# One core of Trainium2: the first ten tiles' work of an attention, MoE and gated-product chain issued in another order

## The chip, the cores and the metric

The kernel runs on one core of one Trainium2 chip. The metric is the device time of one execution in microseconds (us); a smaller one is better. The engines are PE (matrix products and transposes; PEld is its weight load), DVE (the vector engine), ACT (the scalar engine), POOL (GpSimd) and SP, which issues most of the transfers. Each of them takes its instructions strictly in the order in which they were handed to it; semaphores tie the engines to each other.

## The reference, cut to what matters

```
kv  = einsum('bhsd,bhse->bhde', k, v)            # 4 batches, 8 heads, 576 rows, head 64
out = einsum('bhsd,bhde->bhse', q, kv)
x   = out / sqrt(mean(out*out) + 1e-6) * g_norm  # per row and head; x is then 2304 x 512
h   = x @ w_in                                   # 512 -> 1024
e   = exp(h - max(h)); solu = h * e / (sum(e) + 1e-9)
y   = layer_norm(solu) * g_ln @ w_out            # 1024 -> 512
return (y @ w_a * (y @ w_b)) @ w_out2            # 512 -> 1536 -> 512
```

## The kernel before, in words

The 2304 rows are 18 tiles of 128. A first stage makes y of all tiles, two more stages (lines 733 and 905) make the gated product and the output by seven products for eight block products. Products run in a format that keeps fewer bits than float32, so each operand is kept as a high part (a cast on ACT) and a low part (the difference, on DVE or POOL), and each product is three matmuls: high by high, high by low, low by high.

The first stage handles tile i in steps, each a short function that issues instructions to one or two engines:

- `kv_product` (token kp, lines 358 and 363) multiplies k and v of a pair of heads on PE; `kv_keep` copies the result out of PSUM, on DVE (kk) or ACT (ka). There are 16 pairs, 4 for each batch; b0.2 means pair 2 of batch 0.
- `q_turn`, `q_keep` (qt, qk, lines 382, 387) transpose q on PE and copy it out on ACT; `o_product` (op, line 396) is q by kv. `o_square` (ACT, line 407), `o_rms` (line 413 on DVE, then ten small instructions on POOL) and `o_scale` (DVE, line 423) make x.
- `x_turn` (PE, line 433), `x_hi` (ACT, line 438) and `x_lo` (DVE, line 443) give x transposed in its two parts.
- `h_product` (hp, lines 462 to 464): 24 matmuls for h, into the one PSUM buffer `ph`. For tile 0 it is cut into eight pieces h0 to h7, one for each block of w_in, h0 to h3 for the first 512 columns and h4 to h7 for the others. `h_max` (DVE, line 469), `h_exp` (ACT, line 475) and `h_solu` (DVE, lines 480 to 484) read `ph`, and only when `h_solu` is done may the next tile's product write it. `h_square` (ACT), `h_norm` (DVE, then POOL) finish the norm.
- `l_turn`, `l_hi`, `l_lo` (PE, ACT, DVE; lines 518, 528, 531) transpose that result, and `y_product` (yp, lines 548 to 550) is w_out by it for two tiles together.

Beside them the weights are narrowed from a 64-bit format. A block rN of 128 x 512 comes by DMA (`fetch`) into one of five places of `ring`; `begin` (token B, or BP where the clamp goes to POOL) reads it on ACT (line 77); `mid` (M for one block, MM for two) runs the clamp and three more DVE instructions for each (lines 82, 97, 103, 108) and then fetches a further block; `end` makes high part and low part, the low one on POOL (token E) or DVE (EV), line 65. Blocks r1 to r8 are w_in, r9 to r16 w_out (tiles `woh`, `wol`), the rest goes to DRAM for the later stages.

What sets the order of all this is a list of tokens. `PROLOGUE` holds the tokens of tiles 0 to 4 and the front of the following ones, interleaved by hand; `+2` means the tile two later. From tile START on, a fixed list `SLOT` (from tile 10 on `LATER`) is run once for each tile.

```python
    run(PROLOGUE)
    for i in range(START, NTILE - 2):
        run(SLOT if i < 10 else LATER, i)
```

Of the kernel before, what the change touches and what calls it, by code (L numbers as in the profile page):

```python
# [21 lines left out]

START = 5
PROLOGUE = """
LK LW B LW M LQ BP LK LK kp B MM EV LW qt kp LN qk LQ kp LW ka EV ka LQ EV B kk M LQ kp ka BP op LK
os B om qt+1 M E B MM E qk+1 op+1 E os+1 ox qt+2 LQ qt+3 xt qk+2 LK xh E op+2 xl B om+1 M qk+3 os+2
EV om+2 ox+1 LK h0 h1 LQ h2 h3 h4 h6 h5 h7 xt+1 BP xh+1 qt+4 kp hm kp xl+1 op+3 he os+3 B ox+2 hs hq
LQ xt+2 LQ B LK LG xh+2 om+3 hn LK MM xl+2 ka hp+1 hm+1 B kp kp ox+3 ka qk+4 he+1 kk ka op+4 qt+5  # L30
hs+1 lt0 xt+3 os+4 qk+5 lh0 om+4 hp+2 E hq+1 E MM ll0 qt+7 lt1 ox+4 hn+1 hm+2 xh+3 LW BP LK lh1 qt+6
he+2 kp xl+3 op+5 hs+2 B kp os+5 hq+2 om+5 hp+3 qk+6 MM hn+2 LK B LQ xt+4 E ka qk+7 kp ka lt0+1 E
lt1+1 xh+4 hm+3 xl+4 he+3 op+6 lh1+1 ox+5 ll1 lh0+1 B hs+3 ll0+1 lt1+2 ka MM os+6 ll1+1 E EV lh1+2
lt0+2 hp+4 BP xt+5 om+6 B EV EV hq+3 lh0+2 hm+4 he+4 ox+6 hn+3 xh+5 yp yp yp xl+5 hs+4 yp ll1+2
ll0+2 hq+4 lt0+3 hn+4 LK B yk lt1+3 lh0+3 yk M yk M ll0+3 lh1+3 ll1+3 BP E yk
"""
SLOT = """
hp hm lt0-1 lt1-1 lh0-1 lh1-1 ll0-1 ll1-1 xt+1 xh+1 xl+1 op+2 he os+2 yp yk hs hq om+2 kp kk qt+3
# [77 lines left out]
def tile_attention_moe(ctx, tc, q, k, v, g_norm, w_in, w_out, g_ln, w_a, w_b, w_out2, out):  # L116
    nc = tc.nc
    B, H, S, D = q.shape
# [4 lines left out]
    NK = DM // P  # L123
# [36 lines left out]
    left, top, right, late, psum = (ExitStack() for _ in range(5))  # L160
# [121 lines left out]
    def fetch():  # L282
        if fetches:
            src = fetches.pop(0)
            n = len(raws_at) % 5
            raws_at.append(n)
            r = ring[n // 3][:, n % 3 * DM:(n % 3 + 1) * DM]
            nc.sync.dma_start(out=r.rearrange("p (k f) -> p k f", k=NK) if len(src.shape) == 3 else r, in_=src)
            raws.append(r)
# [4 lines left out]
    def begin(on_pool=False):  # L294
        if jobs and raws:
            _, put, args = jobs.pop(0)
            n = Narrow(nc, raws.pop(0), cv.tile([P, DM], U32, tag="u", name="nu"))
            if on_pool:
                n.clamp(nc.gpsimd)
            begun.append((n, put, args))  # L300

    def mid(count=1):
        now = [begun.pop(0) for _ in range(min(count, len(begun)))]
        Narrow.finish([n for n, _, _ in now])
        for n, put, args in now:
# [61 lines left out]
    def kv_keep(copy=nc.vector.tensor_copy):  # L367
        if kvps:
            b, hp, pk = kvps.pop(0)
            for n in range(2):  # L370
                ns = slice(n * D, (n + 1) * D)
                copy(kvb[b % 3][ns, hp, ns], pk[ns])
            ready.add((b, hp))
# [37 lines left out]
    def o_rms(i, eng=nc.gpsimd):  # L411
        ss = sm.tile([P, H], F32, name="ss")
        nc.vector.tensor_reduce(out=ss, in_=sqs.pop(i), op=ALU.add, axis=AX.X)
        ms = sm.tile([P, H], F32, name="ms")
        nc.vector.tensor_scalar(out=ms, in0=ss, scalar1=1.0 / D, scalar2=1e-6, op0=ALU.mult, op1=ALU.add)
        rms[i] = rsqrt(ms, H, "a", eng)

    xt = {}
# [31 lines left out]
    hs_ = {}  # L450

    def h_product(i, part=slice(None)):
        if i not in hs_:
            hs_[i] = dict(ps=ps_h.tile([P, 2, HALF], F32, tag="h", name="ph"))
            hs_[i]["ph"] = hs_[i]["ps"].rearrange("p a b -> p (a b)")
        ph = hs_[i]["ps"]
        xh, xl = xT[i]
        order = [(n, c) for n in range(2) for c in range(NK)]
        order = order if i == 0 else sorted(order, key=lambda nc_: nc_[1])
        for n, c in order[part]:  # L460
            wh, wl = wi[n, c]
            nc.tensor.matmul(ph[:, n, :], xh[:, c, :], wh, start=(c == 0), stop=False)  # L462
            nc.tensor.matmul(ph[:, n, :], xh[:, c, :], wl, start=False, stop=False)  # L463
            nc.tensor.matmul(ph[:, n, :], xl[:, c, :], wh, start=False, stop=(c == NK - 1))  # L464

    def h_max(i):
        d = hs_[i]
# [46 lines left out]
    def l_turn(i, n):  # L514
        pt = ps_t.tile([P, 4, P], F32, tag="t", name="ltp")
        for m in range(4):
            f = 4 * n + m
            nc.tensor.transpose(pt[:, m, :], hs_[i]["so"][:, f * P:(f + 1) * P], ident)  # L518
        psum_of["l", i, n] = pt
# [7 lines left out]
    def l_hi(i, n):  # L527
        nc.scalar.copy(l_part(i, n, 0), psum_of["l", i, n])

    def l_lo(i, n):  # L530
        nc.vector.tensor_tensor(
            out=l_part(i, n, 1), in0=psum_of.pop(("l", i, n)), in1=l_part(i, n, 0).bitcast(F32), op=ALU.subtract
        )
        if (i, n) == ((i // G1 + 1) * G1 - 1, 1):
            pend.extend((i // G1, c) for c in range(NK))
# [476 lines left out]
    def load_gl(_):  # L1012
# [57 lines left out]
    i = NTILE - 2  # L1070
# [8 lines left out]
    i = NTILE - 1  # L1079
# [38 lines left out]
    for n, (count, which) in enumerate(((1, now), (6, later), (5, now), (2, later))):  # L1118
# [3 lines left out]
        for _ in range(count):  # L1122
            part, n = which.pop(0)
# [18 lines left out]
    for j in range(1, NJ - 1):  # L1142
        n = 2 * j + 2
# [181 lines left out]
```

## Time and profile before

| what | value |
|---|---|
| time, median of 3 runs | 688.7 us (688.04 to 689.72) |
| span of the profiled execution, first to last instruction | 686.5 us |
| PE busy in it | 660.6 us, 96% |
| DVE, ACT, POOL busy | 519.4, 283.5, 274.6 us |
| granted PE clock, mean | 0.995 of full |
| chain that ended last, share of PE | 87% |

The page shows one execution, whose time outside the profiler isn't listed apart; its span is 2.2 us under the median of the runs. Of the span cut into 40 equal slices, PE is busy in tenths `3789999999999999999999999999999999999998`: the idle time lies at the front. A wait is put down to the instruction that ended it.

### The profile page before, as it was taken

How to read it: one execution, taken by the hardware profiler on the slowest of the kernel's cores; microseconds unless marked ns; L12 is line 12 of the kernel's file. 1: busy time of each engine (PE TensorE's matmuls, PEld its weight loads, DVE VectorE, ACT ScalarE, POOL GpSimd, SP SyncE). 2: the span in 40 equal slices, each digit the busy share in tenths (PEclk: the TensorE clock that was granted, in tenths of full speed). 3: DMA queues.
4: the chain of work that ended last, by engine and by line, in shares of the span. 5: the costliest groups of instructions: out<-in, count | busy, mean ns of one | idle time of the engine just before them, and what ended most of it. 6: DMA issues, size and time to landing. Idle time of an engine off the chain costs nothing.

```text
span 686.5 us, 12566 instructions
## 1 busy us (share of the span) xinstructions
PE 660.6 (96%) x4710; PEld 634.1 (92%) x4710; DVE 519.4 (76%) x930; ACT 283.5 (41%) x493; POOL 274.6 (40%) x444
## 2 busy tenths in 40 slices
PE   3789999999999999999999999999999999999998
PEld 2668798999999999999999999999999999999997
DVE  4889977675688877879666777686767989978882
ACT  3558854444455346543321122221222545433531
POOL 2667554555534411314564466554672230000000
PEclk9899999999999999999999999999999999999999
DMA  9994745445542412342434346545344784644521
GB/s 304 320 298 137 212 126 182 135 134 161 162 135 70 147 47 70 108 139 89 145 113 150 108 120 199 161 139 150 108 129 135 268 273 141 187 124 139 150 74 62
DMA packets 111100, 103.84 MB, mean 151 GB/s; under 512 B 29248, under 2 KB 98368, under 8 KB 111040
## 3 DMA queue, kind: packets, MB, share of 16 engines
q1 hardware_dynamic: 104992, 94.40, 45.5%
q10 hardware_dynamic: 6048, 8.65, 3.8%
q8 instruction: 37, 0.61, 0.4%
q14 instruction: 23, 0.19, 0.1%
HBM read 71.05 MB, written 31.98 MB: 150 GB/s over the span
## 4 chain that ended last, share of the span: by engine, by line
PE 87%; DVE 5%; DMA 3%; issue 1%; ACT 1%; POOL 1%; SPq 1%; DVEq 0%; ACTq 0%; POOLq 0%
PE pw L733 37%; PE pq L905 19%; PE x2p L550 5%; PE x2p L548 5%; PE x2p L549 5%; PE ph L462 4%; PE ph L463 4%; PE ph L464 4%; DMA ring<-in_moe_w_in_dram 2%; PE ltp L518 2%; PE po L396 2%; PE qtp L382 1%; DMA qs<-in_q_dram 1%; PE xtp L433 1%; DVE nu L103 1%
## 5 line engine op out<-in xcount | busy, mean ns | idle before, releaser
L733 PE MATMUL pw<-xh,wh 128*128 128x384 f32 x336 | 112.9, 336 | 0.8 <-DVE b L785 0.5
L733 PE MATMUL pw<-xh,wl 128*128 128x384 f32 x336 | 112.7, 335 | 0.0
L733 PE MATMUL pw<-xl,wh 128*128 128x384 f32 x336 | 112.6, 335 | 0.0
L775 POOL TENSOR_TENSOR a<-b,a 128x384 f32<-128x384 f32 x53 | 64.4, 1229 | 120.3 <-DVE b L764 120.3
L733 PE MATMUL pw<-x,wh 128*128 128x384 f32 x336 | 85.5, 335 | 0.0
L548 PE MATMUL x2p<-lh,woh 128*128 128x256 f32 x288 | 82.4, 286 | 0.0
L550 PE MATMUL x2p<-lh,wol 128*128 128x256 f32 x288 | 80.4, 279 | 0.8 <-DVE wol L65 0.8
L549 PE MATMUL x2p<-ll,woh 128*128 128x256 f32 x288 | 80.3, 279 | 0.0
L733 PEld LDWEIGHTS pw<-xh,wh 128*128 128x128 f32 x336 | 63.1, 188 | 1.5 <-DVE b L785 0.8
L733 PEld LDWEIGHTS pw<-xl,wh 128*128 128x128 f32 x336 | 63.1, 188 | 0.0
L733 PEld LDWEIGHTS pw<-xh,wl 128*128 128x128 f32 x336 | 63.1, 188 | 0.0
L733 PEld LDWEIGHTS pw<-x,wh 128*128 128x128 f32 x336 | 60.6, 188 | 0.0
L462 PE MATMUL ph<-wih,xh 128*128 128x512 f32 x144 | 56.8, 395 | 2.0 <-DVE so L484 1.8
L905 PE MATMUL pq<-wo,gh 128*128 128x256 f32 x336 | 57.7, 276 | 0.0
L463 PE MATMUL ph<-wil,xh 128*128 128x512 f32 x144 | 56.3, 391 | 0.2 <-DVE wil L65 0.2
L464 PE MATMUL ph<-wih,xl 128*128 128x512 f32 x144 | 56.2, 391 | 0.1
L733 PE MATMUL pw<-x,wl 128*128 128x384 f32 x168 | 56.2, 335 | 0.0
L550 PEld LDWEIGHTS x2p<-lh,wol 128*128 128x128 f32 x288 | 54.5, 189 | 1.2 <-DVE wol L65 1.2
L548 PEld LDWEIGHTS x2p<-lh,woh 128*128 128x128 f32 x288 | 54.2, 188 | 0.3 <-ACT xh L438 0.2
L549 PEld LDWEIGHTS x2p<-ll,woh 128*128 128x128 f32 x288 | 54.2, 188 | 0.0
L905 PE MATMUL pq<-wo,gw 128*128 128x256 f32 x450 | 53.1, 276 | 0.0
L905 PEld LDWEIGHTS pq<-wo,gw 128*128 128x128 f32 x450 | 52.0, 188 | 0.0
(160 smaller groups left out, 1504.0 us busy)
## 6 DMA issues: line engine op xcount, KB each, us to landing
gd<-a SPq DMA_DIRECT2D x72, 192.0 KB, 2.0
ring<-in_moe_w_out_dram SPq DMA_DIRECT2D x20, 512.0 KB, 5.1
gl<-gd SPq DMA_DIRECT2D x14, 384.0 KB, 3.3
gw<-gd SPq DMA_DIRECT2D x12, 384.0 KB, 3.2
ks<-in_k_dram SPq DMA_DIRECT2D x8, 512.0 KB, 5.8
vs<-in_v_dram SPq DMA_DIRECT2D x8, 512.0 KB, 6.3
ring<-in_moe_w_in_dram SPq DMA_DIRECT2D x8, 512.0 KB, 7.4
qs<-in_q_dram SPq DMA_DIRECT2D x16, 256.0 KB, 6.3
```

What stands on the lines that cost most here:

```text
L103: self.nc.vector.scalar_tensor_tensor(out=self.u, in0=self.high, scalar=0xC0000000, in1=self.u, op0=ALU.bitwise_and, op1=ALU.bitwise_or)
L396: nc.tensor.matmul(po[a:a + n, 2 * hp:2 * hp + 2, :], qT[i][:, hp, a:a + n], kvb[b % 3][:, hp, :], start=True, stop=True,)
L462: nc.tensor.matmul(ph[:, n, :], xh[:, c, :], wh, start=(c == 0), stop=False)
L463: nc.tensor.matmul(ph[:, n, :], xh[:, c, :], wl, start=False, stop=False)
L464: nc.tensor.matmul(ph[:, n, :], xl[:, c, :], wh, start=False, stop=(c == NK - 1))
L518: nc.tensor.transpose(pt[:, m, :], hs_[i]["so"][:, f * P:(f + 1) * P], ident)
L548: nc.tensor.matmul(pa, wh[:, cs], lh[:, f, :], start=(f == 0), stop=False)
L549: nc.tensor.matmul(pa, wh[:, cs], ll[:, f, :], start=False, stop=False)
L550: nc.tensor.matmul(pa, wl[:, cs], lh[:, f, :], start=False, stop=(f == NF1 - 1))
L733: nc.tensor.matmul(out, wt_[:, wn, c], xt_[xn][:, c], start=first and c == n == 0, stop=c == 1 and n == 2, skip_group_check=not first,)
L775: eng.tensor_tensor(out=a[n], in0=by, in1=a[n], op=ALU.mult)
L905: nc.tensor.matmul(ps, xt_[:, c], wt_[:, c], start=first and c == n == 0, stop=c == NJ - 1 and n == 2, skip_group_check=not first,)
```

## The change

The token list `PROLOGUE` is a new one that runs up to tile 9 (START is 10), so that `SLOT` is no longer used; the steps themselves are the same and each runs as often as before. The list can't be read for what it moves, so a line of it stands for all. In `h_product` the first matmul on each half of `ph` clears it and the last one closes it, whichever blocks these are, because the new list takes tile 0's pieces as h0 h3 h1 h6 h2 h4 h5 h7.

```diff
-START = 5
+START = 10
 PROLOGUE = """
-LK LW B LW M LQ BP LK LK kp B MM EV LW qt kp LN qk LQ kp LW ka EV ka LQ EV B kk M LQ kp ka BP op LK
+LK LW B LW BP M LK LQ kp LK EV B LW LN qt qk kp MM LQ LW ka EV kp ka EV kk kp B M LQ LQ ka BP op os
...
+        left_ = hs_[i].setdefault("left", [NK, NK])
         for n, c in order[part]:
             wh, wl = wi[n, c]
-            nc.tensor.matmul(ph[:, n, :], xh[:, c, :], wh, start=(c == 0), stop=False)
+            nc.tensor.matmul(ph[:, n, :], xh[:, c, :], wh, start=(left_[n] == NK), stop=False)
             nc.tensor.matmul(ph[:, n, :], xh[:, c, :], wl, start=False, stop=False)
-            nc.tensor.matmul(ph[:, n, :], xl[:, c, :], wh, start=False, stop=(c == NK - 1))
+            left_[n] -= 1
+            nc.tensor.matmul(ph[:, n, :], xl[:, c, :], wh, start=False, stop=(left_[n] == 0))
```

The line numbers of the changed kernel are 8 higher up to `h_product` and 10 higher behind it.

First place, ACT, from tile 0's square (`sq`) on. Block r6 is `nu_290` before and `nu_313` after, r7 `nu_323` and `nu_321`, r8 `nu_388` and `nu_378`; the first `qT` is tile 1's, `xh` is tile 0's. Before:

```order
L407 ACTIVATE sq_288<-po_279 128x512
L77 ACTIVATE nu_290<-ring_114 128x512
L64 CAST wih0_3_319<-nu_252 128x512
L77 ACTIVATE nu_323<-ring_114 128x512
L64 CAST wih1_0_335<-nu_276 128x512
L387 COPY qT_339<-qtp_310 128x512
L64 CAST wih1_1_346<-nu_290 128x512
L407 ACTIVATE sq_350<-po_341 128x512
L387 COPY qT_371<-qtp_354 128x512
L438 ACTIVATE xh_375<-xtp_366,gn_136 128x512
L64 CAST wih1_2_377<-nu_323 128x512
L77 ACTIVATE nu_388<-ring_114 128x512
```

And of the change:

```order
L415 ACTIVATE sq_284<-po_279 128x512
L72 CAST wih0_3_309<-nu_263 128x512
L85 ACTIVATE nu_313<-ring_114 128x512
L395 COPY qT_315<-qtp_286 128x512
L85 ACTIVATE nu_321<-ring_114 128x512
L72 CAST wih1_0_323<-nu_276 128x512
L415 ACTIVATE sq_349<-po_337 128x512
L395 COPY qT_356<-qtp_342 128x512
L72 CAST wih1_1_358<-nu_313 128x512
L85 ACTIVATE nu_378<-ring_114 128x512
L446 ACTIVATE xh_382<-xtp_362,gn_136 128x512
L72 CAST wih1_2_384<-nu_321 128x512
```

Tile 1's `qT` went ahead of the read of r7, and the read of r8 ahead of tile 0's `xh`; r7's high part stays behind `xh`.

Second place, DVE, behind the narrowing of r6 and r7, around the first tile's `x` and `xl`. Before:

```order
L108 SCALAR_TENSOR_TENSOR nu_323<-ring_114,nu_323 128x512
L423 TENSOR_TENSOR x_352<-po_279,y_a_296 128x512
L443 SCALAR_TENSOR_TENSOR xl_386<-xtp_366,gn_136,xh_375 128x512
L413 TENSOR_REDUCE ss_390<-sq_350 128x8
L415 TENSOR_SCALAR ms_392<-ss_390 128x8
L210 TENSOR_SCALAR y_a_394<-ms_392 128x8
L82 TENSOR_SCALAR nu_388<-nu_388 128x512
```

And of the change:

```order
L116 SCALAR_TENSOR_TENSOR nu_321<-ring_114,nu_321 128x512
L431 TENSOR_TENSOR x_347<-po_279,y_a_295 128x512
L73 TENSOR_TENSOR wil1_2_385<-nu_321,wih1_2_384 128x512
L451 SCALAR_TENSOR_TENSOR xl_390<-xtp_362,gn_136,xh_382 128x512
L421 TENSOR_REDUCE ss_408<-sq_349 128x8
L423 TENSOR_SCALAR ms_410<-ss_408 128x8
L218 TENSOR_SCALAR y_a_412<-ms_410 128x8
L90 TENSOR_SCALAR nu_378<-nu_378 128x512
```

The low part of r7 came from POOL, and stands on DVE between `x` and `xl`.

Third place, DVE, from the last narrowing instruction ahead of tile 3's `h_max` (`nm`) to tile 3's `h_solu` (`so`). Before:

```order
L108 SCALAR_TENSOR_TENSOR nu_836<-ring_115,nu_836 128x512
L501 TENSOR_SCALAR va_909<-vs_851 128x1
L210 TENSOR_SCALAR y_l_911<-va_909 128x1
L469 TENSOR_REDUCE nm_975<-ph_871 128x1
L443 SCALAR_TENSOR_TENSOR xl_977<-xtp_931,gn_136,xh_973 128x512
L423 TENSOR_TENSOR x_988<-po_825,y_a_857 128x512
L531 TENSOR_TENSOR ll_696<-ltp_769,lh_695 128x4x128
L480 TENSOR_SCALAR rs_994<-se_980 128x1
L481 RECIPROCAL rs_994<-rs_994 128x1
L484 SCALAR_TENSOR_TENSOR so_997,su_998<-ph_871,rs_994,e_979 128x1024
```

And of the change:

```order
L116 SCALAR_TENSOR_TENSOR nu_867<-ring_115,nu_867 128x512
L73 TENSOR_TENSOR wol2_942<-nu_533,woh2_941 128x512
L479 TENSOR_REDUCE nm_946<-ph_869 128x1
L73 TENSOR_TENSOR wol3_951<-nu_578,woh3_950 128x512
L431 TENSOR_TENSOR x_966<-po_818,y_a_842 128x512
L541 TENSOR_TENSOR ll_697<-ltp_782,lh_696 128x4x128
L451 SCALAR_TENSOR_TENSOR xl_989<-xtp_935,gn_136,xh_978 128x512
L490 TENSOR_SCALAR rs_991<-se_986 128x1
L491 RECIPROCAL rs_991<-rs_991 128x1
L494 SCALAR_TENSOR_TENSOR so_994,su_995<-ph_869,rs_991,e_985 128x1024
```

Two low parts of w_out (r11 and r12) came from POOL; ahead of this piece a kv copy-out and one more clamp came to DVE too, and the small `va` and `y_l` moved further ahead.

## Rows read from the trace of the kernel before

**Rows 1.** Busy time by stretch: us, then PE, PEld, DVE, ACT, POOL, granted clock, DMA

```profile
core 0: us, PE busy (x) PEld busy (x) DVE busy (x) ACT busy (x) POOL busy (x), PEclk, DMA share, GB/s
0.00:37.00 37.00, 19.90 (x148) 16.48 (x148) 23.93 (x45) 17.05 (x32) 18.65 (x38) 0.91 0.97 307
37.00:90.00 53.00, 48.57 (x402) 41.52 (x402) 48.30 (x100) 38.91 (x75) 34.82 (x92) 1.00 0.67 198
90.00:540.00 450.00, 449.72 (x2953) 434.50 (x2953) 329.70 (x627) 166.97 (x298) 210.80 (x310) 1.00 0.44 133
```

**Rows 2.** Waits of PE from 37 to 90 us: engine, line, waited for, us, times, longest

```profile
PE ph L462 <- DVE so L484: 1.8, 3, 0.9
PE xtp L433 <- DVE x L423: 0.9, 1, 0.9
PE x2p L550 <- DVE wol L65: 0.8, 1, 0.8
```

**Rows 3.** Timeline of PE to 37 us: start, us, instruction, idle before and what ended it

```profile
22.19 1.09 PE L382 MATMUL qtp<-ident,qs 128*128 128x128 f32 x4 [2.89 <-DMA qs<-in_q_dram]
...
30.91 0.50 PE L464 MATMUL ph<-wih,xl 128*128 128x512 f32 x1
...
34.88 0.39 PE L463 MATMUL ph<-wil,xh 128*128 128x512 f32 x1
...
36.46 0.50 PE L463 MATMUL ph<-wil,xh 128*128 128x512 f32 x1 [0.23 <-DVE wil L65]
```

**Rows 4.** Timeline of ACT, 23 to 31 us

```profile
23.42 0.68 ACT L77 ACTIVATE nu<-ring 128x512 f32<-128x512 f32 x1 [1.72 <-DMA ring<-in_moe_w_in_dram]
...
24.50 0.59 ACT L387 COPY qT<-qtp 128x512 f32<-128x512 f32 x1
...
29.97 0.61 ACT L64 CAST wih<-nu 128x512 fp32r<-128x512 f32 x1
```

**Rows 5.** Timeline of DVE, 27 to 39 us

```profile
27.68 0.69 DVE L423 TENSOR_TENSOR x<-po,y_a 128x512 f32<-128x512 f32 x1
30.11 0.75 DVE L443 SCALAR_TENSOR_TENSOR xl<-xtp,gn,xh 128x512 fp32r<-128x512 f32 x1 [1.73 <-ACT xh L438]
...
31.48 1.10 DVE L415 TENSOR_SCALAR ms<-ss 128x8 f32<-128x8 f32 x1
32.62 0.17 DVE L210 TENSOR_SCALAR y_a<-ms 128x8 int32<-128x8 int32 x1
...
35.72 0.69 DVE L65 TENSOR_TENSOR wil<-nu,wih 128x512 fp32r<-128x512 f32 x1 [0.69 <-ACT wih L64]
...
37.95 1.22 DVE L469 TENSOR_REDUCE nm<-ph 128x1 f32<-128x1024 f32 x1
```

**Rows 6.** Timeline of DVE, 50 to 60 us

```profile
50.19 0.45 DVE L372 COPY kvb<-kvp 64x64 f32<-64x64 f32 x2
...
53.61 0.76 DVE L82 TENSOR_SCALAR nu<-nu 128x512 f32<-128x512 f32 x2
...
58.99 1.21 DVE L469 TENSOR_REDUCE nm<-ph 128x1 f32<-128x1024 f32 x1
```

**Rows 7.** Timeline of PE, 63 to 84 us

```profile
63.37 0.47 PE L462 MATMUL ph<-wih,xh 128*128 128x512 f32 x1 [0.88 <-DVE so L484]
...
74.03 0.47 PE L462 MATMUL ph<-wih,xh 128*128 128x512 f32 x1 [0.23 <-DVE so L484]
...
83.27 0.39 PE L550 MATMUL x2p<-lh,wol 128*128 128x256 f32 x1 [0.81 <-DVE wol L65]
```

**Rows 8.** Timeline of DVE, 69 to 79 us

```profile
69.10 1.23 DVE L469 TENSOR_REDUCE nm<-ph 128x1 f32<-128x1024 f32 x1 [0.65 <-PE ph L464]
...
76.38 2.38 DVE L103 SCALAR_TENSOR_TENSOR nu<-ring,nu 128x512 uint32<-128x512 uint32 x2
```

**Rows 9.** Timeline of DVE, 65 to 67 us, the same two instructions

```profile
65.70 1.29 DVE L103 SCALAR_TENSOR_TENSOR nu<-ring,nu 128x512 uint32<-128x512 uint32 x2
```

**Rows 10.** Timeline of POOL, 76 to 79 us

```profile
76.90 1.31 POOL L65 TENSOR_TENSOR wol<-nu,woh 128x512 fp32r<-128x512 f32 x1 [1.73 <-ACT woh L64]
```

**Rows 11.** Busy time by stretch, columns as in the first group

```profile
20.00:30.00 10.00, 5.95 (x32) 5.58 (x32) 8.17 (x17) 5.08 (x10) 7.12 (x13) 0.66 1.06 335
```

More of the change, by code (lines that the diff above doesn't have):

```diff
@@ L21 @@
 LINE = 16
-START = 5
+START = 10
 PROLOGUE = """
-LK LW B LW M LQ BP LK LK kp B MM EV LW qt kp LN qk LQ kp LW ka EV ka LQ EV B kk M LQ kp ka BP op LK
[L28 to L35, printed above, removed]
+LK LW B LW BP M LK LQ kp LK EV B LW LN qt qk kp MM LQ LW ka EV kp ka EV kk kp B M LQ LQ ka BP op os
+qt+1 om E B qk+1 M B E MM op+1 qt+2 ox os+1 qt+3 qk+2 E xt LK op+2 LK B LQ xh EV os+2 xl LK h0 h3 h1
@@ new lines @@
+qk+3 om+1 M EV h6 om+2 h2 ox+1 LQ h4 h5 BP h7 xt+1 kp hm xh+1 he ox+2 hs xl+1 op+3 B os+3 qt+4 kp BP
+LQ om+3 ka xt+2 hq xh+2 MM xl+2 B hp+1 kp hn hm+1 kp ox+3 LK qk+4 ka ka kk he+1 LQ op+4 qt+5 LG LK
+xt+3 lt0 hs+1 os+4 qk+5 lh0 hp+2 hq+1 om+4 E E MM kp ll0 qt+7 xh+3 lt1 qt+6 LW hn+1 hm+2 xl+3 LK
+ox+4 op+5 he+2 B hs+2 os+5 hq+2 om+5 kp B hp+3 kk hn+2 qk+6 LK MM LQ lt1+1 xt+4 lh1 EV hm+3 qk+7 EV
+kp ox+5 BP ka op+6 xh+4 lt0+1 he+3 ll1 xl+4 hs+3 lh1+1 lh0+1 B MM E lt1+2 ll0+1 ka ll1+1 os+6 lh1+2
@@ new lines @@
+lt0+2 EV hp+4 BP xt+5 lh0+2 BP om+6 EV EV hm+4 hq+3 he+4 ox+6 hn+3 xh+5 yp xl+5 yp hs+4 yp ll1+2 yp
+yk B lt1+3 hq+4 hn+4 lt0+3 lh0+3 ll0+2 BP yk yk M M ll0+3 hp+5 LQ xt+6 lt0+4 hm+5 lh1+3 lt1+4 lh0+4
+lh1+4 ll1+3 ll0+4 ll1+4 op+7 xh+6 xl+6 he+5 hs+5 yp os+7 hq+5 om+7 kp E hp+6 hn+5 kk EV qt+8 LQ qk+8
+yp yk MM BP yk BP yk ox+7 LK hm+6 lt1+5 lt0+5 lh1+5 ll1+5 kp xt+7 xh+7 LK op+8 he+6 os+8 EV yp lh0+5
+ll0+5 om+8 BP qt+9 ka yk EV hs+6 hq+6 xl+7 qk+9 hn+6 MM yp hp+7 ox+8 op+9 lt0+6 BP hm+7 os+9 lt1+6
@@ L36 @@
+LK lh1+6 ll1+6 lh0+6 EV E xt+8 ll0+6 xh+8 kp xl+8 LK he+7 yp hs+7 hq+7 qt+10 qk+10 om+9 LQ yk yk MM
+hn+7 yp BP ox+9 B hp+8 yk E kp LK lt0+7 lt1+7 lh0+7 hm+8 E kk lh1+7 ll1+7 xt+9 op+10 xh+9 xl+9 ll0+7
+he+8 os+10 om+10 qt+11 yp hs+8 LQ hq+8 qk+11 hn+8 yp yk MM hp+9 EV kk ox+10 BP LQ hm+9 lt0+8 lt1+8
+lh1+8 xt+10 qt+12 xh+10 BP op+11 he+9 yp ll1+8 os+11 hs+9 lh0+8 E yk om+11 hq+9 yk yp xl+10 hn+9 kp
+MM qk+12 E BP ll0+8 BP LK yk kk ox+11
 """
```

## The prediction

> **What bounds the kernel now.** I read the stretches first [rows 1]. From 90 to 540 us PE is busy for 449.72 of 450 us: whatever is issued there in another order can't gain, since nothing is idle. That takes tiles 6 to 9, which is most of what the longer list adds, out of the sum. The idle time that this change can reach lies ahead of 90 us: 37 - 19.90 = 17.1 us up to 37 us and 53 - 48.57 = 4.4 us from 37 to 90 us. Whatever shift PE has at its first y product (about 80 us) it carries to the end, because from there on it never waits long enough to make up for it.
>
> Next the waits of PE in the second stretch [rows 2]. All three name DVE: the next tile's h product waits until `h_solu` has read `ph` (1.8 us in three waits), a transpose waits for x (0.9), a y product for a low part of w_out (0.8). DVE is busy for 48.30 of those 53 us, nearly as much as PE. So up to 90 us DVE is the engine to follow: a step that comes to DVE ahead of `h_max` or `h_solu` delays PE, one that leaves it helps.
>
> In the first stretch the timelines tell what the first h product waits for. Its third matmul (30.91 us) needs tile 0's `xl`, and its 23rd (36.46 us) stood 0.23 us for the low part of the last block, r8 [rows 3]. `xl` itself hangs on x (27.68 us) [rows 5], which stands on DVE behind the narrowing of r6 and r7, and that on ACT's read of r7, which waited 1.72 us for the transfer [rows 4].
>
> **The change part by part.**
>
> *Order of transfers.* Batch 0's remaining rows of k and v go ahead of q of tile 0 instead of behind it. PE's first 16 groups are in the same order as before, and the same bytes stand ahead of q of tile 1 and of r7, so I leave their landing where it was. PE's transpose of q of tile 1 began at 22.19 us, straight from its transfer, and took 1.09 us [rows 3]. The earlier start of tile 0's square and root hides behind the narrowing of r6 and r7: nothing.
>
> *Tile 0's x.* On ACT tile 1's `qT` (0.59 us) now stands ahead of the read of r7. It can't begin before 22.19 + 1.09 = 23.28 us and ends near 23.9 us, so r7 is read at 23.9 instead of 23.42 us [rows 3, 4]. DVE's pair and x behind it: +0.5 us, x at 28.2. Bounds: 0 (q lands sooner) to 0.6 (a whole copy).
>
> *Tile 0's xl.* `xl` came 30.11 - 27.68 = 2.43 us after x [rows 5]. Now r7's low part stands between them on DVE. It needs r7's high part, which ACT makes only behind `xh`: 0.61 us [rows 4], then the subtraction, 0.69 us as for r8's [rows 5]; starts are about 0.1 us closer than durations, so +1.2. `xl` begins at 28.2 + 2.43 + 1.2 = 31.8 us instead of 30.11, and the third matmul, 0.80 us behind, at 32.6 instead of 30.91. From the third to the 20th matmul PE took (34.88 - 30.91) / 17 = 0.23 us each [rows 3]; the 23rd comes at 32.6 + 20 x 0.234 = 37.3 us, against 36.46: **+0.8 us**. The order h0 h3 h1 h6 by itself gains nothing: all blocks but r8 are there by then, and h7 is last in both.
>
> *Does r8 come later still?* From `xl` to r8's low part DVE took 35.72 - 30.11 = 5.61 us, in which one `ms` took 1.10 us where a row of its size takes 0.17 [rows 5]. POOL was then doing the low part of r7, which has left it. Without that, 31.8 + 5.61 - 0.93 = 36.5, and the 23rd matmul 0.74 us behind at 37.2: it meets PE's 37.3. If `ms` is held again, +1.7. I take +0.8, since the instruction beside it is gone. `h_max` of tile 0 followed r8's low part by 37.95 - 35.72 = 2.23 us: 38.7, +0.8.
>
> *Tiles 1 and 2.* Tile 1's `xl` (0.75) moves behind tile 0's `h_solu`; ahead of tile 2's `h_max` x (0.69) and one clamp (0.76 / 2 = 0.38) leave DVE [rows 5, 6]. These cancel within 0.4 us, and as that `h_max` (58.99 us) also waits for a product that starts 0.8 us late at most, I put it at +0.3, and with it tile 3's product at 63.37 us, which waits for DVE [rows 6, 7]. Bounds 0 and +0.8.
>
> *Tile 3.* Ahead of its `h_max` DVE gets a kv copy-out (0.45), a clamp (0.38) and the low part of r11 (0.69): 1.5 us [rows 5, 6]. DVE had 0.65 us of idle time there [rows 8], so `h_max` is 0.3 + 1.5 - 0.65 = 1.2 us late. Between it and `h_solu` the low part of r12 adds 0.6: +1.8 us, and the next h product waits for exactly that `h_solu` (74.03 us) [rows 7]: PE +1.8.
>
> *First y product.* Before, it stood 0.81 us for the low part of r15 [rows 7], and some 0.25 for r16. It now comes 1.8 us later, while DVE has a clamp less and POOL fewer subtractions beside it, so both waits go: 1.8 - 1.07 = **+0.7 us**. Work that PE then does without a gap carries this to the end.
>
> Sum: 688.7 + 0.7 = **689.4 us** (the profiled span 686.5 + 0.7 = 687.2, and the 2.2 us by which the median lies above it).
>
> *A rule against this.* The two DVE instructions that took 2.38 us at 76.38 us took 1.29 at 65.70 [rows 8, 9]; at 76.90 POOL ran a subtraction of 1.31 us [rows 10]. The Trainium skill, "SBUF — State Buffer", section "SBUF: two separate sides", says that the two engines take a port pair as a lock for a whole instruction, so that the second one stands. Those rows agree. By that rule each subtraction taken from POOL gives DVE back about what it costs there. That is the first rival.
>
> **The rivals.**
>
> 1. *DVE gets back what POOL took.* A subtraction on POOL cost DVE 2.38 - 1.29 = 1.09 us in that pair [rows 8, 9] and `ms` 0.93 [rows 5]; three subtractions leave POOL (r7, r11, r12), so up to 3 x 1.09 = 3.3 us, against 3 x 0.69 = 2.1 for doing them. If also x isn't late, the waits for DVE (3.5 us, rows 2) shrink by two thirds: -2.3, 686.4 us. Against it: r7's wait for ACT stays whatever POOL does, and only two of the moved subtractions lay beside a long pair. Chance 0.18.
> 2. *Little moves.* Half of rival 1 meets half of the costs: 686.7 to 688.7 us, say 688.0. Chance 0.21.
> 3. *DVE is late at tile 3 and nothing is given back* (slower). The place is `h_max` and `h_solu` of tile 3. If `ms` is held (+0.9) and the y product still waits for r15 and r16 (1.07), it is 0.7 + 0.9 + 1.07 = +2.7: 691.4 us. It decides from the point where DVE's pair r15 and r16 ends over 0.6 us after the y product's matmul that needs it. Chance 0.10.
> 4. *The low clock reaches into the h product.* From 20 to 30 us the granted clock is 0.66 on average, so the lower level (1.2 GHz) holds for about two thirds of it, behind PE's waits, and it is full again when the product runs [rows 11, 1]. PE's new stall ahead of the third matmul could hold it low: half of 24 matmuls at twice 0.234 us is +2.8, with the 0.7: 692.2 us. Chance 0.06.
>
> **How the numbers follow.** The forecast has 0.45, for 688.7 to 690.7 us. About 0.3% (2.1 us) is what a measurement of this kernel can tell from no change; its runs differ by 1.7 us. Faster by more than that is rival 1, 0.18; slower rivals 3 and 4, 0.16; within it the forecast and rival 2, 0.66. The range goes from rival 1's 686.4 to rival 3's 691.4; beyond it lie rival 4 and tails on either side.
>
> **What would show it.** Right: r7 read by ACT behind `qT`; PE standing over 1 us ahead of the first product's third matmul, for `xl`; the 23rd near 37.3; the fifth h product waiting over 1 us for `h_solu`; no wait for `wol` at 80 to 90 us. Wrong: `xl` by 31 us, the fifth h product before 74.5 us, or a wait over 0.5 us behind 100 us, where batch 3's rows of k and v are now asked for later.

## The result: 692.2 us, slower by 0.56%

The changed kernel takes **692.2 us** (median of 6 runs, 690.19 to 693.12), the kernel before 688.14 (6 runs beside it): ratio 1.0056 [1.0042, 1.0070], the brackets being a 95% interval. That is 4.06 us more, where 0.7 was forecast: 692.2 lies above the 689.4 that was forecast and above the range, which ended at 691.4. The profiled execution of the change took 692.02 us with a span of 690.2, against 686.5 for the span before.

Starts of h products on PE and of the later stages, in us, from the timelines of PE (tiles count from 0, so tile 5's is the sixth h product):

| | before | after | shift |
|---|---|---|---|
| tile 1's h product | 42.70 | 43.49 | +0.79 |
| tile 4's h product | 74.03 | 75.86 | +1.83 |
| tile 5's h product | 93.55 | 94.31 | **+0.76** |
| tile 7's h product | 123.08 | 126.00 | +2.92 |
| tile 8's h product | 137.64 | 141.42 | +3.78 |
| tile 12's h product | 194.52 | 199.06 | **+4.54** |
| second stage, first matmul | 278.45 | 282.99 | +4.54 |
| last stage, first matmul | 553.52 | 557.27 | +3.75 |

The second stage is the same code in all these kernels, yet it took 273.8 to 275.2 us in the profiles of this study (275.07 in that of before, 274.28 in that of the change), so the last 0.8 us of the table is scatter. The first 0.8 us is what the forecast had. The 3.8 us between tile 5's and tile 12's product is where it had nothing. The table is of one execution each; the experiments tell how far it holds.

Busy time by stretch of the changed kernel, columns as in [rows 1]:

```profile
0.00:37.00 37.00, 18.70 (x145) 15.70 (x146) 23.62 (x45) 17.19 (x32) 17.11 (x35) 0.91 0.96 300
37.00:90.00 53.00, 49.08 (x399) 40.82 (x399) 48.56 (x101) 39.02 (x75) 34.85 (x93) 1.00 0.65 201
90.00:540.00 450.00, 447.19 (x2934) 430.88 (x2933) 325.10 (x617) 164.61 (x292) 212.63 (x309) 1.00 0.44 131
```

From 90 to 540 us PE is now busy for 447.19 us instead of 449.72: a stretch that stood idle for 0.3 us now stands for 2.8. Which waits these are the waits of PE from 93 to 200 us tell (engine, line, waited for: us, times, longest). Before:

```profile
PE ltp L518 <- POOL so L506: 0.3, 1, 0.3
```

After:

```profile
PE kvp L371 <- DMA vr<-in_v_dram: 1.6, 1, 1.6
PE ltp L528 <- POOL so L516: 1.0, 4, 0.3
PE x2p L558 <- DVE ll L541: 0.2, 1, 0.2
```

Two things are new: a kv product waits for a transfer, and four transposes of a tile's norm (`ltp`) instead of one wait for POOL's last instruction of that norm (`so`). That is 2.8 - 0.3 = 2.5 us of gaps. The same 780 matmuls lie between the two h products before and after, so the whole shift between them, 3.8 us, is lost time. A gap costs more than it shows: in an undisturbed row matmuls last 0.39 us and start 0.23 apart, so each begins 0.16 us before the one ahead of it ends, and that overlap is lost at a wait as well. Five more waits by 0.16 us are 0.8, so by this estimate 3.3 of the 3.8 us is accounted for; what the rest is isn't shown.

In the first 40 us the main events came when they were forecast. DVE:

```profile
26.14 2.37 DVE L116 SCALAR_TENSOR_TENSOR nu<-ring,nu 128x512 uint32<-128x512 uint32 x2
28.54 0.69 DVE L431 TENSOR_TENSOR x<-po,y_a 128x512 f32<-128x512 f32 x1
31.21 0.69 DVE L73 TENSOR_TENSOR wil<-nu,wih 128x512 fp32r<-128x512 f32 x1 [1.98 <-ACT wih L72]
31.82 0.74 DVE L451 SCALAR_TENSOR_TENSOR xl<-xtp,gn,xh 128x512 fp32r<-128x512 f32 x1
...
36.50 0.69 DVE L73 TENSOR_TENSOR wil<-nu,wih 128x512 fp32r<-128x512 f32 x1 [0.69 <-ACT wih L72]
...
38.74 1.21 DVE L479 TENSOR_REDUCE nm<-ph 128x1 f32<-128x1024 f32 x1
```

PE, the third matmul of tile 0's product, and where tile 4's product waits:

```profile
32.62 0.50 PE L474 MATMUL ph<-wih,xl 128*128 128x512 f32 x1 [1.16 <-DVE xl L451]
...
75.86 0.47 PE L471 MATMUL ph<-wih,xh 128*128 128x512 f32 x1 [0.44 <-DVE so L494]
```

`xl`, r8's low part and `h_max` come at 31.82, 36.50 and 38.74 us (forecast 31.8, 36.5, 38.7), the third matmul at 32.62 (32.6). Tile 3's `h_solu` starts at 74.42 instead of 72.60 us. The product behind it waits 0.44 us for it, not the over 1 us that the prediction named as a sign: two transposes ahead of that product stood 0.63 and 0.76 us already. Of its delay of 1.83 us 0.53 were there at tile 3's product, and the rest is spread over these three waits.

### The profile page after: what moved, and what is told of

It reads as the page before. It is cut to its first block, busy times and chain, and to the rows that moved or that the text cites. A ratio compares the mean times of both kernels' runs of the same rounds, so it can differ in the third digit from the quotient of the medians.

```text
span 690.2 us, 12566 instructions
## 1 busy us (share of the span) xinstructions
PE 661.7 (96%) x4710; PEld 633.6 (92%) x4710; DVE 519.3 (75%) x932; ACT 283.4 (41%) x493; POOL 275.4 (40%) x442
## 4 chain that ended last, share of the span: by engine, by line
PE 83%; DVE 7%; DMA 3%; SPq 2%; POOL 2%; issue 2%; ACT 1%; POOLq 0%; DVEq 0%; ACTq 0%
PE pw L743 37%; PE pq L915 19%; PE x2p L558 4%; PE x2p L560 4%; PE x2p L559 4%; PE ph L471 3%; PE ph L474 3%; PE ph L472 3%; PE ltp L528 2%; PE po L404 1%; DMA qs<-in_q_dram 1%; SPq L334 1%; DVE so L494 1%; DMA kr<-in_k_dram 1%; DMA vr<-in_v_dram 1%
```

## The experiments

Theory A after the first look: the front costs about what was forecast, and the rest of the loss is made in tiles 5 to 9, part of it by the later load of batch 3's remaining rows of k and v and part by late norms. Its rivals stand in the expectations.

**1. Only the front, or only the tiles behind it.** One kernel has the new tokens of tiles 0 to 4 and `SLOT` from tile 5 on (x1_front):

```diff
-START = 10
+START = 5
...
-yk B lt1+3 hq+4 hn+4 lt0+3 lh0+3 ll0+2 BP yk yk M M ll0+3 hp+5 LQ xt+6 lt0+4 hm+5 lh1+3 lt1+4 lh0+4
...
+yk B lt1+3 hq+4 hn+4 lt0+3 lh0+3 ll0+2 BP yk yk M M ll0+3 lh1+3 ll1+3 E yk LK
```

> The new list's order for tiles 0 to 4 alone, then the fixed list of before for tiles 5 to 9; the remaining rows of batch 3 are asked for at the end of the front. Theory A (the loss lies in tiles 5 to 9, above all in the late request for batch 3's remaining rows, and the front costs the 0.8 us that PE shows at tile 5's product): tile 5's product begins 0.8 us later than before, no wait of PE over 0.3 us from 95 to 180 us, time 0.6 to 1.0 us over before. Theory B (the front's heavier load on DVE leaves tiles 5 to 9 short of slack, so waits follow whatever list runs there): waits of over 1 us in sum from 95 to 180 us, time 3 to 4 us over before.

The other has the old tokens of tiles 0 to 4, and the new ones behind (x2_tail), with the load of batch 3's rows where it was before.

> The order of before for tiles 0 to 4, then the new list's order for tiles 5 to 9, with batch 3's remaining rows asked for where before has it. Theory A: tile 5's product begins as before (93.6 us), the wait for those rows (1.6 us) is absent, and the short waits for the norm on POOL remain: time 0.5 to 1.5 us over before. Theory B: no difference from before, within 0.4 us.

Measured: 688.46 us for the front alone, 1.0012 [1.0001, 1.0023], and 689.9 for the later tiles alone, 1.0026 [1.0014, 1.0038], beside 688.06 for the kernel before. So the front costs 0.4 and the tiles behind it 1.8 us, with about 0.8 us of uncertainty on each: theory A, with the front somewhat under its figure and the later tiles over it. The profiles tell the two apart more sharply. With the front alone PE does the 780 matmuls from tile 5's to tile 12's product in 100.97 us, as before, so the new front does not make the later tiles wait (theory B). With the later tiles alone it takes 102.80 us and stands at the same places as the change (start, us, instruction, wait):

```profile
113.70 1.09 PE L528 MATMUL ltp<-ident,so 128*128 128x128 f32 x8 [0.20 <-POOL so L516]
129.98 1.09 PE L528 MATMUL ltp<-ident,so 128*128 128x128 f32 x8 [0.29 <-POOL so L516]
132.47 0.39 PE L558 MATMUL x2p<-lh,woh 128*128 128x256 f32 x1 [0.23 <-DVE ll L541]
...
159.06 1.09 PE L528 MATMUL ltp<-ident,so 128*128 128x128 f32 x8 [0.22 <-POOL so L516]
```

The kernel before has none of these four waits. Counted from start to start, against the same step of PE where it doesn't wait, they cost about 0.36, 0.45, 0.43 and 0.37 us, together 1.6 of the 1.83 us (an estimate from these profiles). That leaves about 0.2 us for PE's own new order, a rival that is named in experiment 5.

**2. Only the load moved back** (e1_rest_early), the rest as in the change:

```diff
-yk B lt1+3 hq+4 hn+4 lt0+3 lh0+3 ll0+2 BP yk yk M M ll0+3 hp+5 LQ xt+6 lt0+4 hm+5
+yk B lt1+3 hq+4 hn+4 lt0+3 lh0+3 ll0+2 BP yk yk M M ll0+3 LK hp+5 LQ xt+6 lt0+4 hm+5
...
-yp yk MM BP yk BP yk ox+7 LK hm+6
+yp yk MM BP yk BP yk ox+7 hm+6
```

> The changed kernel with one token moved: batch 3's remaining rows of k and v are asked for before tile 5's product instead of behind the fetch of two more weight blocks. Theory A: the wait of the kv product (1.6 us) goes, and with it some of the waits behind it: 1.6 to 2.2 us less than the changed kernel, so 1.9 to 2.5 us over before. Theory B: PE finds another wait in its place (for the norm or for DVE) and gains less than 0.5 us.

Measured: 690.42 us, 1.0037 [1.0024, 1.0051], 2.36 us over the kernel before where the change is 4.06 over it: 1.7 us gained, theory A. The wait for `vr` is gone, those for the norm stay, and the 780 matmuls take 103.04 us instead of 104.74 in the change, 1.7 us less as well. Front, load and later tiles add up to 0.4 + 1.7 + 1.8 = 3.9 of the 4.06 us by which the change is slower; with about 1 us of uncertainty on each term, that they fit so well is partly luck. How the load came so late SP's queue shows (start, us, instruction). Before:

```profile
80.92 0.63 SPq L335 DMA_DIRECT2D kr<-in_k_dram  x1
81.60 0.63 SPq L335 DMA_DIRECT2D vr<-in_v_dram  x1
```

After, with the two instructions ahead of it and the kv product:

```profile
110.70 0.38 SPq L296 DMA_DIRECT2D ring<-in_moe_w_b_dram  x1
111.30 0.34 SPq L296 DMA_DIRECT2D ring<-in_moe_w_out_dram  x1
111.69 0.63 SPq L343 DMA_DIRECT2D kr<-in_k_dram  x1
112.36 0.63 SPq L343 DMA_DIRECT2D vr<-in_v_dram  x1
```

```profile
118.02 0.34 PE L371 MATMUL kvp<-vr,kr 128*64 128x64 f32 x4 [1.56 <-DMA vr<-in_v_dram]
```

The load stands in SP's queue behind two fetches of blocks into `ring`, which can go only when DVE has narrowed the blocks that lay there. It goes out 31 us later than before, and PE's product comes 5.66 us behind it.

**3. Two low parts of w_out back on POOL** (e2_low_pool): is it DVE's load at tile 3 that counts?

```diff
-ox+4 op+5 he+2 B hs+2 os+5 hq+2 om+5 kp B hp+3 kk hn+2 qk+6 LK MM LQ lt1+1 xt+4 lh1 EV hm+3 qk+7 EV
+ox+4 op+5 he+2 BP hs+2 os+5 hq+2 om+5 kp B hp+3 kk hn+2 qk+6 LK MM LQ lt1+1 xt+4 lh1 E hm+3 qk+7 E
```

> The changed kernel with the low parts of r11 and r12 and the clamp of r13 back on POOL, as before had them. Theory A (these are what delayed tile 3's h_solu, but the first y product hid most of it): tile 4's product at 74.5 us instead of 75.9, the first y product waits about 1 us for r14 to r16 again, and the total is 0 to 0.6 us less than the changed kernel. Rival (what is saved at tile 4 stays saved): 1.0 to 1.5 us less.

Measured: 693.46 us, 1.0084 [1.0067, 1.0101], 5.4 us over the kernel before where the change is 4.06 over it. Neither expectation. Tile 4's product did come earlier, at 74.44 us instead of 75.86, but the first y product later, at 82.23 instead of 81.79:

```profile
73.56 1.09 PE L528 MATMUL ltp<-ident,so 128*128 128x128 f32 x8 [0.90 <-POOL so L516]
82.23 0.35 PE L558 MATMUL x2p<-lh,woh 128*128 128x256 f32 x1 [1.62 <-DVE ll L541]
```

On DVE `ll` stands behind a narrowing pair that waited for its clamp on POOL, and POOL did that behind the two subtractions:

```profile
76.79 1.86 DVE L105 TENSOR_SCALAR nu<-nu 128x512 uint32<-128x512 uint32 x2 [0.51 <-POOL nu L90]
```

So `h_solu` of tile 3 is not the only gate of the first y product; what POOL got came back on the other path. In this profile tile 5's product is 0.63 us later than in the change, and behind it the kv product's wait for `vr` is 1.96 us instead of 1.56, which adds 0.4 us.

**4. r7's low part back on POOL**, in the whole change (e3_r7_pool) and in the front alone (w1_front_pool):

```diff
-qk+1 M B E MM op+1 qt+2 ox os+1 qt+3 qk+2 E xt LK op+2 LK B LQ xh EV os+2 xl LK h0 h3 h1
+qk+1 M B E MM op+1 qt+2 ox os+1 qt+3 qk+2 E xt LK op+2 LK B LQ xh E os+2 xl LK h0 h3 h1
```

> The changed kernel, with the low part of block r7 of w_in made on POOL again instead of DVE. Theory A (the subtraction of 0.69 us between tile 0's x and xl is what makes xl late): tile 0's xl begins at once behind xh, near 30.7 us instead of 31.82, and the first h product's third matmul near 31.5 instead of 32.6. The 23rd matmul gains less, since r8's low part comes behind POOL's subtraction again: tile 0's h_max 0 to 0.8 us earlier than 38.74, and the first y product as before it. Time 691.4 to 692.2 us. Rival B (xl is late because x is, and the subtraction fills time in which DVE waits anyway): xl stays within 0.3 us of 31.8.

> The changed order of tiles 0 to 4 with the fixed list behind it (688.46 us), and r7's low part on POOL. Theory A (that subtraction between x and xl is what the first tiles' order loses on DVE): the second h product starts 1.1 us earlier than with it on DVE at the same start of the first, the sixth 0.4 us ahead of the kernel before's (93.55 us); 687.6 to 688.0 us where the kernel before takes 688.0. Rival B (xl is late because x is): no difference from 688.46 us.

The whole change: 693.25 us, 1.0085 [1.0063, 1.0107], no saving. Its four executions were 691.20, 691.50, 695.01 and 695.42 us; the profiled one took 695.01, and in it x came a microsecond later than in the change (29.52 us) and the granted clock was 0.50 from 32 to 34 us. In it `xl` follows x by 2.18 us instead of 3.28, which is theory A's step; the time says nothing about it, because most of what this execution lost lies elsewhere. Its 780 matmuls took 106.42 us instead of 104.74: the late load again, with a wait of 2.50 us, and behind it the granted clock was 0.50 (the 1.2 GHz level) from 120 to 122 us (PE, then columns as in [rows 1]):

```profile
119.22 0.34 PE L371 MATMUL kvp<-vr,kr 128*64 128x64 f32 x4 [2.50 <-DMA vr<-in_v_dram]
```

```profile
120.00:122.00 2.00, 2.00 (x17) 1.67 (x17) 0.00 (x0) 1.37 (x2) 0.00 (x0) 0.50 0.88 324
```

The front alone: **687.74 us**, beside 687.77 for the kernel before, 0.9999 [0.9990, 1.0009]. Its profile, DVE and PE:

```profile
27.15 0.69 DVE L423 TENSOR_TENSOR x<-po,y_a 128x512 f32<-128x512 f32 x1
29.31 0.75 DVE L443 SCALAR_TENSOR_TENSOR xl<-xtp,gn,xh 128x512 fp32r<-128x512 f32 x1 [1.47 <-ACT xh L438]
...
37.42 1.21 DVE L471 TENSOR_REDUCE nm<-ph 128x1 f32<-128x1024 f32 x1
```

```profile
42.17 0.47 PE L463 MATMUL ph<-wih,xh 128*128 128x512 f32 x1 [0.31 <-ACT kvb L372]
```

Tile 1's product starts 1.1 us before that of x1_front (43.26), tile 5's at 93.09 us instead of 93.88. These are theory A's numbers, though not all owed to the subtraction: in x1_front's profile the clock fell too (last section). The times alone can't tell the two kernels apart, 0.9999 and 1.0012 with intervals of 0.0010 and 0.0011 on either side. Of all kernels here this is the only one whose median isn't above that of the kernel before, and it is no faster.

A further step from there, r8's narrowing ahead of tile 1's root, and tile 1's x and one `BP` behind tile 0's `h_max` (w2_r8_early):

```diff
-qk+3 om+1 M EV h6 om+2 h2 ox+1 LQ h4 h5 BP h7 xt+1 kp hm xh+1 he ox+2 hs xl+1
+qk+3 M om+1 EV h6 om+2 h2 LQ h4 h5 h7 kp hm ox+1 xt+1 he BP xh+1 ox+2 hs xl+1
```

> As the one before, and the narrowing of r8 directly behind tile 0's xl, ahead of tile 1's root, with tile 1's x behind tile 0's h_max. If the end of tile 0's product hangs on r8's low part, h_max of tile 0 comes 0.3 to 0.6 us earlier, and with it the h products up to the fifth; the first y product then gains as much or waits for w_out's low parts. 687.2 to 687.9 us. If tile 1's x, now late, holds the second tile: the second and third h product 0.5 to 1 us later, 688.3 to 688.9 us.

Measured: 689.42 us, 1.0021 [1.0011, 1.0032]. The second and third h product come 1.0 us later than in w1_front_pool (43.21 and 53.79 us), as in the second expectation, but by another cause, and the time is above its range. Tile 0's product now waits 1.23 us for r8's high part:

```profile
36.19 0.50 PE L463 MATMUL ph<-wih,xh 128*128 128x512 f32 x1 [1.23 <-ACT wih L64]
```

On ACT that cast stands behind a square (`sq`) that waited 4.87 us for DVE. Here a step brought forward on DVE gained nothing, because its partner on ACT stayed where it was.

**5. The norms of tiles 6 and 8**, three tries on x2_tail, with PE's order unchanged. First the root of x of tiles 8 and 10 back behind `h_solu` (t1_root_behind):

```diff
-ll0+5 om+8 BP qt+9 ka yk EV hs+6 hq+6 xl+7 qk+9 hn+6 MM yp hp+7
+ll0+5 BP qt+9 ka yk EV hs+6 hq+6 om+8 xl+7 qk+9 hn+6 MM yp hp+7
...
-he+8 os+10 om+10 qt+11 yp hs+8 LQ hq+8 qk+11 hn+8
+he+8 os+10 qt+11 yp hs+8 LQ hq+8 om+10 qk+11 hn+8
```

> The kernel with the first five tiles' order of before and the changed order of tiles 5 to 9 (689.9 us), in which for tiles 8 and 10 the root of x (token om) stands behind h_solu and h_square of tiles 6 and 8 again, as the fixed list has it. Theory C (the late norms come from where their small POOL instructions fall: beside DVE's pair of narrowing instructions of 1.28 us each they take 1.1 to 1.5 us instead of 0.2 to 0.35): with POOL busy at the root first, the norms of tiles 6 and 8 start later but run behind the pair, end no later than before, and PE's waits for so at 129.98 and 159.06 us go; 689.0 to 689.6 us. Rival D (it is the amount of POOL work ahead of the norm): the norms end 1 to 2 us later, PE's waits for so grow to over 1 us each, 691 to 693 us.

Measured: 689.65 us, 1.0038 [1.0025, 1.0051], no better than x2_tail. The norm's small instructions did speed up. In x2_tail, tile 6's norm on POOL, and DVE's pair beside it:

```profile
124.50 1.53 POOL L224 TENSOR_SCALAR p_l<-y_l,va 128x1 f32<-128x1 f32 x1
126.14 1.10 POOL L224 TENSOR_SCALAR t_l<-p_l 128x1 f32<-128x1 f32 x1
127.34 0.27 POOL L224 TENSOR_SCALAR y_l<-t_l,y_l 128x1 f32<-128x1 f32 x1
```

```profile
124.71 1.27 DVE L111 SCALAR_TENSOR_TENSOR nu<-ring,nu 128x512 uint32<-128x512 uint32 x2
125.91 1.28 DVE L116 SCALAR_TENSOR_TENSOR nu<-ring,nu 128x512 uint32<-128x512 uint32 x2
```

In t1_root_behind:

```profile
126.44 0.34 POOL L224 TENSOR_SCALAR p_l<-y_l,va 128x1 f32<-128x1 f32 x1
126.88 0.27 POOL L224 TENSOR_SCALAR t_l<-p_l 128x1 f32<-128x1 f32 x1
```

They start 1.9 us later and the norm ends at the same time, 129.81 against 129.92 us. Theory C had the durations and the end right, and not what PE makes of it: its waits for `so` do not go, they add up to 1.4 us instead of 1.0. The root's instructions now run beside the pair instead, and there some take 0.53 us, where they took 0.20 in x2_tail.

The second try puts `h_exp`, `h_solu` and `h_square` of tiles 6 and 8 ahead of `l_hi` and `l_lo` steps of the tile before (t2_solu_early); the third moves `h_exp` and `h_solu` of tile 6 alone, leaves `h_square` in place and puts the norms of both tiles ahead of the root on POOL (t3_norm_first). Tile 6's tokens of the third:

```diff
-hm+6 lt1+5 lt0+5 lh1+5 ll1+5 kp xt+7 xh+7 LK op+8 he+6 os+8 EV
+hm+6 he+6 lt1+5 lt0+5 lh1+5 ll1+5 hs+6 kp xt+7 xh+7 LK op+8 os+8 EV
-yp lh0+5 ll0+5 om+8 BP qt+9 ka yk EV hs+6 hq+6 xl+7 qk+9 hn+6 MM
+yp lh0+5 ll0+5 BP qt+9 ka yk EV hq+6 xl+7 qk+9 hn+6 om+8 MM
```

> The kernel with the first five tiles' order of before and the changed order of tiles 5 to 9 (689.9 us), in which h_exp and h_solu of tiles 6 and 8 stand on ACT and DVE ahead of the l_hi and l_lo steps of the tile before that they stood behind, and the norm of tiles 6 and 8 on POOL ahead of the root of tiles 8 and 10. PE's order is the same. Theory G (in the changed order h_solu of tile 6 waits in DVE's queue behind an l_lo that itself waits 3.2 us for PE and ACT, and the norm behind it comes too late): h_solu of tile 6 by 116 us instead of 120.91, PE's waits for so at 129.98 and 159.06 us and for ll at 132.5 us go, the tenth h product comes 0.5 to 0.8 us earlier against the sixth; 689.1 to 689.4 us. Rival H (PE's own order costs it, by more changes between kinds of product): PE's time from the sixth to the twelfth h product stays within 0.2 us, 689.9 us.

> The kernel with the first five tiles' order of before and the changed order of tiles 5 to 9 (689.9 us), in which the norm of tiles 6 and 8 stands on POOL ahead of the root of tiles 8 and 10, and h_solu of tile 6 on DVE ahead of the last l_lo of tile 5; unlike the earlier try, h_square of tile 6 stays on ACT behind the copy-out of kv that PE waited for there. PE's order is the same. Theory G (the norms of tiles 6 and 8 are late because of what stands ahead of them in DVE's and POOL's queues): PE's waits for so at 129.98 and 159.06 us go, the tenth h product starts 0.7 us earlier against the sixth, and the span from the sixth to the thirteenth h product is 101.6 to 102.1 us (100.97 before, 102.80 with the changed order of these tiles); 688.7 to 689.3 us. Rival I (these tiles have so little slack that another wait takes the place of each one removed, as in the earlier try): 102.6 us or more, 689.7 to 690.5 us.

Measured: 691.4 us, 1.0055 [1.0039, 1.0071], and 692.54 us, 1.0060 [1.0042, 1.0077]. In both the waits for `so` at tiles 6 and 8 are gone, and larger ones stand elsewhere. Second try, PE and, for its cause, ACT:

```profile
123.03 0.38 PE L558 MATMUL x2p<-lh,woh 128*128 128x256 f32 x1 [1.58 <-ACT kvb L380]
```

```profile
119.34 1.15 ACT L502 ACTIVATE e<-so,su 128x1024 f32<-128x1024 f32 x1 [2.40 <-DVE so L494]
```

`h_square` waited 2.40 us on ACT for `h_solu`, and kv's copy-out was queued behind it. Third try, PE:

```profile
132.02 0.63 PE L441 MATMUL xtp<-ident,x 128*128 128x128 f32 x4 [1.26 <-DVE x L431]
...
162.47 0.63 PE L441 MATMUL xtp<-ident,x 128*128 128x128 f32 x4 [1.57 <-DVE x L431]
```

Now the root is behind the norm on POOL and x comes late: rival I. In this order PE wants the norm of one tile and x of another within about two microseconds of each other, and POOL makes both, one after the other. That is shown; that no other order of these tiles could serve both isn't. None of the three tries lowered the 1.8 us, so that the waits for the norms make up most of it rests on the profile of x2_tail (experiment 1) and not on an edit that won it back. Rival H is bounded there too: about 0.2 us are left for it.

**6. One subtraction moved from POOL to DVE in the kernel before** (n2_low_dve): the port rule of the prediction by itself.

```diff
-lt1+1 xh+4 hm+3 xl+4 he+3 op+6 lh1+1 ox+5 ll1 lh0+1 B hs+3 ll0+1 lt1+2 ka MM os+6 ll1+1 E EV lh1+2
+lt1+1 xh+4 hm+3 xl+4 he+3 op+6 lh1+1 ox+5 ll1 lh0+1 B hs+3 ll0+1 lt1+2 ka MM os+6 ll1+1 EV EV lh1+2
```

> The kernel before, with one low part of w_out (the subtraction of 1.31 us on POOL at 76.90 us, beside DVE's pair of narrowing instructions that took 2.38 and 1.73 us) made on DVE behind that pair. Theory E (each of the two engines stands while the other's instruction is under way, so POOL's subtraction costs DVE more than doing it): the pair takes 1.29 and 1.29 us, DVE gains 1.53 and pays 0.69, the low part that the first y product waits for comes 0.8 us earlier, PE's wait of 0.81 us at 83.27 us shrinks under 0.3; 687.2 to 687.6 us. Rival F (DVE's long pair has another cause, for instance the reads of its source on ACT): the pair stays at 2.4, the wait grows by 0.7 to 1.5 us, 688.7 us.

Measured: 688.54 us beside 687.49, 1.0012 [1.0002, 1.0022], no faster, and outside theory E's range. DVE:

```profile
76.23 1.28 DVE L103 SCALAR_TENSOR_TENSOR nu<-ring,nu 128x512 uint32<-128x512 uint32 x2
77.44 1.28 DVE L108 SCALAR_TENSOR_TENSOR nu<-ring,nu 128x512 uint32<-128x512 uint32 x2
```

The first two took 2.38 us [rows 8] and take 1.28, the other two 1.73 and 1.28: on the pair theory E is right. The Trainium skill, "SBUF — State Buffer", section "SBUF: two separate sides", says that a DVE instruction with two inputs and a POOL one take the port pair that they share for a whole instruction, while the other is blocked; the trace agrees. PE's wait of 0.81 us [rows 7] broke into three short ones, of 0.20 us for `woh` from ACT and 0.24 and 0.22 for `wol`, and tile 5's product starts at 93.50 us, against 93.55. ACT is next in line there: DVE itself waits 0.40 and 0.56 us for `woh`.

**7. Three of the edits at once** (m1_mended): the load of experiment 2, the root of t1_root_behind and r7's low part on POOL.

> The changed kernel with three edits at once: batch 3's remaining rows of k and v loaded ahead of tile 5's h product, the root of x of tiles 8 and 10 behind h_solu as in the fixed list, and r7's low part on POOL. Theory A and C: the losses add up, so that the parts mended (1.8, 0.3 to 0.9 and 0 to 0.8 us) come off 692.2: 688.9 to 690.1 us. Rival D: the second edit costs what the others save, 690.5 us or more.

Measured: 690.51 us, 1.0045 [1.0031, 1.0058], about what the load alone gave (690.42), on the border of rival D. The median stands between two groups, three executions at 689.3 to 689.5 us and three at 691.5 to 691.8, whose cause isn't known; so it is only shown that the other two edits gave nothing clear on top. The waits for `so` in it add up to 1.4 us instead of 1.0.

## Why the prediction was wrong

- *Transfers, x, xl, r8* (+0.8): right. r7 was read a little sooner than forecast (23.19 us instead of 23.9), because q landed sooner, but the last two instructions of the narrowing ahead of x took 2.37 us instead of 1.29 beside POOL's subtractions; the two nearly cancelled, and that `xl` came at the very time is luck.
- *Tiles 1 to 3* (+1.8 at tile 4's product): right in size, 1.83; tile 3's product was 0.53 late instead of 0.3, and the sign, a wait of over 1 us for `h_solu`, came as 0.44.
- *First y product* (+0.7): right; 0.76 at tile 5's product, with no wait for `wol` left. The closeness is partly luck: in other profiles with the same front that product is 0.33 us (x1_front) or 2.13 us (e1_rest_early) later than before.
- *What rows 2 name*: "All three name DVE" holds for the three longest waits; the same view of the kernel before has three shorter ones, of which one, of 0.5 us, is for POOL and one, of 0.2 us, for ACT.
- **The step that failed** stands ahead of the sum: "whatever is issued there in another order can't gain, since nothing is idle. That takes tiles 6 to 9, which is most of what the longer list adds, out of the sum." That PE is busy for 449.72 of 450 us excludes a gain and not a loss. It says that the old order of these tiles made every wait come out at nothing, not that there was slack. The runs showed in its place that the new order of tiles 5 to 9 costs 1.8 us by itself (x2_tail), by the profile mostly in waits for norms, and the later load 1.7 more (e1_rest_early).
- "Whatever shift PE has at its first y product ... it carries to the end" failed with it: 0.76 became 4.54.
- *Order of transfers*: priced for batch 0 alone. The text named batch 3's rows as a sign of error ("a wait over 0.5 us behind 100 us") and gave them no price. SP's order showed the load behind two fetches, which wait for DVE; their time went into no term.
- *Rival 1*: its mechanism is real (experiment 6), its gain didn't come. In that experiment the time returned to DVE met a wait for ACT.
- *Rivals 3 and 4*: neither is what happened in the profile of the change, where the clock stayed at full through tile 0's product. Rival 4's 692.2 us is the measured time by chance. Its clock did fall in four other profiles with the new front (below).

## What to carry to other kernels

A stretch in which the bounding engine never waits has hardly anything to gain by a new order, and it can lose, so its steps belong into the sum with a price of nothing or more: list, for each wait that is now nothing, who arrives last and how late it may come. In a load, look for what stands ahead of it in the issuing queue and on which engine that waits. Engines that work in order pass a wait on: three edits that were to remove waits of 0.2 to 0.3 us (w2_r8_early, t2_solu_early, t3_norm_first) made ones of 1.2 to 1.6 us elsewhere.

## What was not expected of the hardware

Two POOL instructions on 128x1 elements that took 0.34 and 0.27 us in t1_root_behind took 1.53 and 1.10 in x2_tail, beside DVE's pair of 1.27 and 1.28 us (experiment 5), four times as long. The norm they belong to is a chain of such instructions on POOL, which grew by 2 us there.

The low clock of rival 4 appeared in the profile of x1_front. There PE stood 1.97 us ahead of the third matmul of tile 0's product, and the granted clock then fell, to 0.50 (the 1.2 GHz level) from 34 to 36 us, in the midst of the product (columns as in [rows 1]):

```profile
32.00:34.00 2.00, 2.00 (x6) 1.62 (x7) 1.86 (x6) 1.07 (x2) 0.81 (x3) 0.71 1.24 268
34.00:36.00 2.00, 2.00 (x6) 1.58 (x5) 1.28 (x3) 0.77 (x2) 1.67 (x5) 0.50 0.88 121
```

Its matmuls took up to 0.63 us instead of 0.39, and `h_max` of tile 0 came at 38.94 us, though x had come 1.4 us sooner (27.11) than in the profile of the change, where PE stood 1.16 us and the clock stayed at full. Without the stall, in w1_front_pool, it was 37.42. The clock was also at 0.50 within this product in the profiles of e2_low_pool (34 to 36 us, behind a standstill of 1.95), e3_r7_pool (32 to 34 us) and e1_rest_early, where it had not risen before the product, which began at 32.81 us instead of 30.72. That makes four of the eight profiles with the new front, and none of the six with the old one. What it adds to the median of the change isn't shown.
